# A third working set for VectorE's exponentials, and the scheduler's pace set anew

## The chip, the cores and the metric

The kernel runs on one core of a Trainium2 chip. The metric is the device time of one execution in microseconds (us); lower is better. The engines are called as in the profile: PE (TensorE), ACT (ScalarE), DVE (VectorE), POOL (GpSimd) and SP (SyncE, which issues all DMAs here).

## The reference

Two layers, each an attention block and a dense block, over one sequence of 2048 tokens of width 448, with weights shared by the layers:

```python
def _A_ref(x, wqkv, wo):          # H = 16 heads of Dh = 28
    qkv = (x @ wqkv).reshape(B, S, 3, H, Dh)...
    scores = jnp.einsum("bhqd,bhkd->bhqk", q, k) * Dh ** -0.5
    p = _softmax(scores, axis=-1)
    o = jnp.einsum("bhqk,bhkd->bhqd", p, v)
    return o.transpose(0, 2, 1, 3).reshape(B, S, D) @ wo

def _B_ref(x, w1, b1, w2, b2):    # F = 1792
    r = jnp.maximum(jnp.einsum("bsd,df->bsf", x, w1) + b1, 0)
    return jnp.einsum("bsf,fd->bsd", r * r, w2) + b2

x = A_x                           # (1, 2048, 448) bf16
x = x + _A_ref(_layernorm(x), A_wqkv, A_wo)
x = x + _B_ref(_layernorm(x), B_w1, B_b1, B_w2, B_b2)
x = x + _A_ref(_layernorm(x), A_wqkv, A_wo)
x = x + _B_ref(_layernorm(x), B_w1, B_b1, B_w2, B_b2)
```

## The kernel before

**Units and groups.** The scores are computed with keys on the partitions. A unit is a 128 x 512 tile of scores of one head in one bank of PSUM: two key blocks of 128 by 256 queries, or four by 128 for the last two query blocks of layer 1. There are 2048 units. `s_stream` takes them in threes; a group's scores (`sc`, 128 x 1536, two buffers) are filled by PE (line 882), and `e_stream` has ACT write their exponentials to a probability tile `pt` in bf16 (line 907; `NPT` = 11 buffers of 128 x 1536). `p_stream` multiplies the probabilities with V into `oT` (line 1057). V's spare columns hold ones, so the row sums come along, and `norm_pair` or `norm_turn` divides by them.

**VectorE's thirds.** Where `apart` allows it, the third unit of a group goes to DVE, and ACT's exponential is 128 x 1024. `a_unit` and `a_rest` need four DVE instructions: take (line 965, scores from PSUM to integers), power (line 980, the exponent part), square and close (lines 987 and 995, the polynomial of the fraction, and the product to bf16). They need a working set. `R_v` holds two: one of tiles of its own (`v_i`, `v_e`, `v_h`), the other in parts of the key tiles that are unused at the time (shown as `K_sb<-K_sb`), where the square is written over the integers. The second is there for query blocks 2 to 6 of layer 0 and for layer 1. The close writes to a buffer outside the group: a tile `pd`, or unused blocks of `V_sb` or tiles `h`; `pd_free` lists them, and `held` counts how many are promised.

**The rest.** An opening computes layernorm, Q, K and V block by block between the first groups (`first_block`; the passes are cut as `OPENING` says). When a query block is done, `chain` runs its output projection, layernorm, both products of the dense block (hidden products at line 606 into `r`, squares, then 14 products with `w2`) and adds the result to `x_sb` (line 1193); layer 0's chain ends in the next layer's Q, K and V, layer 1's in a store (line 1281). `heat` puts products with an identity on PE (line 1311), and `s_stream` repeats score products, where PE would otherwise have little to do.

**What sets the order.** Nothing is ordered at run time. A planner keeps modelled clocks for the engines, and from all streams takes again and again the operation that could start first (the order of the streams' priorities on a tie). So constants change the order of instructions on every engine. The constants that count here: `BUSY` and `LOW` (the modelled share of DVE, over `SPAN` us, above which no third is given to it), `TB` and `TB2` (the same for its backlog), `behind` with `L0E`, `L0N`, `L1E`, `L1N` and `MARGIN` (how far the chains must have come by a given unit; when they are behind, the tighter limits hold), `NEAR`, `KEEP`, `LAG` (when banks are left to the chains, when a late third is waited for, where in a pass it may be taken from).

Of the kernel before, what the change touches and what calls it, by code (L numbers as in the profile page):

```python
# [39 lines left out]
OWN = 2  # L40
HALF = 320
L0E = 1310
L0N = 7.6
L1E = 1980
L1N = 6.2
MARGIN = 3.5
LOW = 0.95
TURNS = 1
ENDU = 100
# [10 lines left out]
WINDOW = 2.8  # L60
C_PRIO = 1.6
V_PRIO = 8.5
V_LATE = 4.6
V_LAST = 3
V_AGE = 6
V_PAST = 5
OWN3 = 0
FIRST = 50
V_FIRST = 9
V_WAIT = 3.5  # L70
NEAR = 6
FAR = 17
KEEP = 5
LAG = 5
LEAD = 15
LAST = 690
BUSY = 1.01
TB = 3.6
TB2 = 0.9
SPAN = 8  # L80
NPT = 11
NOS = 2
AEND = 0
# [153 lines left out]
def kernel(  # L237
# [34 lines left out]
    vp = ctx.enter_context(tc.tile_pool(name="vp", bufs=1))  # L272
    osp = ctx.enter_context(tc.tile_pool(name="osp", bufs=NOS))
    np_ = ctx.enter_context(tc.tile_pool(name="np_", bufs=2))
    sp = ctx.enter_context(tc.tile_pool(name="sp", bufs=6))
    dp = ctx.enter_context(tc.tile_pool(name="dp", bufs=NOS, space=bass.MemoryType.DRAM))
    ps_sc = ctx.enter_context(tc.tile_pool(name="ps_sc", bufs=2, space=bass.MemoryType.PSUM))
    ps_m = [ctx.enter_context(tc.tile_pool(name=f"ps_m{i}", bufs=1, space=bass.MemoryType.PSUM)) for i in range(2)]
# [4 lines left out]
    R_r, R_xt, R_os, R_xn, R_on, R_rec = Res(2), Res(3), Res(NOS), Res(2), Res(2), Res(2)  # L283
    R_h = [Res(2), Res(2)]

    R_v = (Res(1), Res(1))


    R_pd = [*[Res(1) for _ in range(5)], Res(NHP), *[Res(1) for _ in range(2)]]
# [476 lines left out]
    def sets_of(unit):  # L766

        pi, kb, r, hh = unit
        l, qb, *_ = passes[pi]
        if l == 0:  # L770
            return R_v if 2 <= qb <= 6 else R_v[:1]
        return R_v

    def apart(i, now, us, soon=SOON):

        if len(units) - i < STOP or not LEAD <= len(gbuf) <= LAST:
            return None
        l, qb = passes[units[i][0]][:2]
        if sum(r.when() is not None and r.when() <= now + soon for r in sets_of(units[i])) <= (0 if soon else pending[0]):
            return None  # L780
        j = i
        if i + LAG > ends_at[units[i][0]]:
            j = ends_at[units[i][0]] + 1
            while j in taken:
                j += 1
            if j >= len(units):
                return None
            rows = {u[3] for u in us}
            js = [k for k in range(j, j + 4) if k < len(units) and k not in taken and units[k][3] not in rows]
            j = js[0] if js else j  # L790
        if passes[units[j][0]][0] != passes[us[0][0]][0]:
            return None
        if held[0] + 1 > min(sum(r.n for r in pd_free(units[k])) for k in (i, j)):
            return None
        if any(pl.tok.get(d) is None or pl.tok[d].end + LAT["DVE"] > now for d in needs(units[j])):
            return None
        if pl.load(SPAN, "DVE") > (LOW if behind(i) else BUSY):
            return None
        if max(0.0, pl.clock["DVE"] - now) + left[0] > (TB2 if behind(i) else TB):
            return None  # L800
        return j
# [16 lines left out]
    def s_stream():  # L818
        while at[0] < len(units):
            gi = len(gbuf)  # L820
            js = ahead(3)
            us = [units[j] for j in js]
            gbuf.append({"n": len(us)})

            def fn(e, gi=gi, us=us, js=js):
                sc = ps_sc.tile([P, 3 * 512], DT.float32, name="sc", tag="sc")
                gbuf[gi]["sc"] = sc
                dst = [sc[:, k * 512:k * 512 + 512] for k in range(len(us))]
                ks = list(range(len(us)))

                def next_at(j):
                    at[0] = j
                    rest = ahead(1)
                    at[0] = rest[0] if rest else len(units)
                    return rest
                own, j = True, None
                if OWN3 and bank_free(o.start) and next_at(js[-1] + 1):
                    j = apart(at[0], o.start, us)
                elif len(us) == 3 and THIRD:
                    own = False  # L840
                    next_at(js[1] + 1)
                    j = apart(at[0], o.start, us[:2], 0.0)
                if j is None:
                    next_at(js[-1] + 1)
                else:
                    if not own:
                        us, ks = us[:2], ks[:2]
                        gbuf[gi]["n"] = 2
                    us, ks = us + [units[j]], ks + [3]
                    taken.add(j)  # L850
                    held[0] += 1
                    pending[0] += 1
                    next_at(at[0])
                    if own:
                        x = gbuf[gi]["x"] = Op("PE", 0.0, None)
                        x.res = min((r for r in R_m if r.when() is not None), key=lambda r: r.when())
                        x.turn = len(x.res.rel)
                        x.res.rel.append(None)
                        dst.append(bank(x, "mt"))
                    else:  # L860
                        x = gbuf[gi]["x"] = o
                        o.need = 2
                    pl.spawn(C_PRIO, a_unit(gi, x, dst[-1], us[-1], passes[us[0][0]][0]))
                for k, (pi, kb, r, hh) in zip(ks, us):
                    where.setdefault((pi, kb), []).append((gi, k, hh))
                    if len(where[pi, kb]) == G:
                        pl.tok["u", pi, kb] = o

                short = (HOT if len(units) - at[0] > ENDU else HOTE) - pl.load(HWIN)
                again = 0  # L870
                if short > 0 and gi > 0:
                    last = ("e" in gbuf[gi - 1] and gbuf[gi - 1]["e"].end) or pl.clock["ACT"] + 1.35
                    again = max(0, min(MORE, int(min(o.room, last - LAT["PE"] - 0.05 - o.end) / 0.22)))
                o.more = 0.22 * again
                for i in list(range(4)) * (again + 1):
                    for k, (pi, kb, r, hh) in enumerate(us):
                        if i >= r:
                            continue
                        l, qb, g, *_ = passes[pi]
                        t0, nt = blocks[l][qb]  # L880
                        rows = slice(DHP * hh, DHP * hh + DHP)
                        nc.tensor.matmul(dst[k][:, i * nt * P:(i + 1) * nt * P],  # L882
                                         lhsT=K_sb[l][rows, g, (kb + i) * P:(kb + i + 1) * P],
                                         rhs=Q_sb[rows, g, t0 * P:(t0 + nt) * P],
                                         start=True, stop=True, tile_position=(DHP * hh, 0))
            o = gbuf[gi]["s"] = Op("PE", 0.20 + 0.01 * max(u[2] for u in us), fn,
                                   deps=list({d for u in us for d in needs(u)}), acq=R_sc, mode="row", sets=("s", gi))
            yield o
        s_left.clear()
        pl.tok["send"] = o  # L890
# [7 lines left out]
    def e_stream():  # L898
        gi = 0
        while gi < len(gbuf) or s_left:  # L900
# [3 lines left out]
            def fn(e, gi=gi, n=n):  # L904
# [3 lines left out]
                                         scale=float(np.log(2.0)) * 2.0 ** -FRAC)  # L908
                if gbuf[gi].get("x") is gbuf[gi]["s"]:
                    apart_from(gi, t)  # L910
            o = gbuf[gi]["e"] = Op("ACT", n / 1200 + 0.066, fn, deps=[("s", gi)], acq=R_pt, need=n // 512,
                                   rel=gbuf[gi]["s"], sets=("e", gi))
            yield o
            gi += 1
# [20 lines left out]
            return V_sb[0][:, 8 + i, :, :].rearrange("p h r -> p (h r)")  # L935
        return hp.tile([P, QB], DT.bfloat16, name="h")[:, :]

    v_i = const.tile([P, 512], DT.int32, name="v_i")
    v_e = const.tile([P, 512], DT.int32, name="v_e")
    v_h = const.tile([P, 512], DT.float32, name="v_h")  # L940

    def set_of(res, l):

        k = R_v.index(res)
        two = lambda a: a.rearrange("p (a n) -> p a n", a=2)
        if k == 0:
            i, e, h = two(v_i[:, :]), two(v_e[:, :]), two(v_h[:, :])
        else:
            keys = K_sb[1 - l][:, :, S - 512:S] if l == 0 else K_sb[0][:, :, 0:512]
            i, e = keys[:, 0:2, :].bitcast(DT.int32), keys[:, 2:4, :].bitcast(DT.int32)  # L950
            h = i.bitcast(DT.float32)
        return i, e, h, two

    def a_unit(gi, x, src, unit, l):
        yield Op("-", 0.0, None, deps=[("s", gi)])
# [19 lines left out]
    def a_rest(gi, c, box, unit):  # L975
# [10 lines left out]
        def square(e):  # L986
            nc.vector.scalar_tensor_tensor(out=box["h"], in0=box["f"], scalar=lin, in1=box["f"],  # L987
                                           op0=ALU.add, op1=ALU.mult)
        h = Op("DVE", 0.684, square, deps=[c] if c.res is R_v[0] else [c, p])
        yield h  # L990
        left[0] -= 0.6

        def close(e):
            pd = gbuf[gi]["pd"] = pd_of(o)
            nc.vector.scalar_tensor_tensor(out=box["two"](pd), in0=box["h"], scalar=low, in1=box["e"].bitcast(DT.float32),  # L995
                                           op0=ALU.add, op1=ALU.mult)
        o = Op("DVE", 0.683, close, deps=[p, h], acq=lambda: pd_free(unit), rel=c, sets=("x", gi))
        gbuf[gi]["x"] = o
        yield o
        left[0] -= 0.6  # L1000
# [6 lines left out]
    def p_stream():  # L1007


        for pi, (l, qb, g, kbs, first, last) in enumerate(passes):  # L1010
# [18 lines left out]
            while todo:  # L1029
# [16 lines left out]
                def fn(e, now=now, begin=begin, close=close, box=box, pi=pi, l=l, g=g, r=r, n=n):  # L1046
                    if "t" not in box:
                        p_next[0] = None
                        box["t"] = bank(box["o"], "oT")
                    held[0] -= sum(k == 3 for kb in now for _, k, _ in where[pi, kb])  # L1050
                    for kb in now:
                        for i in range(r):
                            for gi, k, hh in where[pi, kb]:
# [10 lines left out]
                o = Op("PE", 0.04 + 0.22 * len(now), fn,  # L1064
                       deps=[*by, *{("V", l, kb + i) for kb in now for i in range(r)}],
                       acq=None if "o" in box else pools_now(),
                       rel=[gbuf[gi][w] for w, gi in by], mode="col")
                box.setdefault("o", o)
                yield o
            if last and quick(l, qb, g):  # L1070
# [291 lines left out]
```

## Time and profile before

| | |
|---|---|
| median of 3 runs | 863.42 us (863.35 to 865.34) |
| the profiled execution | 863.88 us, of which its span is 862.1 us |
| granted TensorE clock | 1.00 over the span |
| busy in the span | ACT 842.1 us, PE 817.5, DVE 797.1, POOL 42.8 |
| DMA | 17.97 MB, mean 21 GB/s |

The span runs from the first to the last instruction; 1.78 us of the profiled execution lie around it. Lines of the profile name a source line, an engine, an operation, the tile written and the tiles read, with sizes in partitions x elements. The busy time of a group is the union of its instructions: where one starts before its neighbour ends, the overlap is counted once, so the mean duration times the count can exceed it.

### The profile page before, as it was taken

The page shows a single profiled execution, that of the slowest core. Times are in us where ns is not written, and L with a number is a line of the kernel's source. Part 1 is how long each engine was busy: PE and PEld are TensorE (multiplying, and loading weights), DVE is VectorE, ACT ScalarE, POOL GpSimd, SP SyncE. Part 2 cuts the span into 40 slices and gives each one's busy share as a digit, 9 for nine tenths or more (in the row PEclk, how much of TensorE's full clock was granted, in tenths as well). Part 3 has the DMA queues.
Part 4 walks back from the last instruction along what each step waited for, and adds up shares of the span by engine and source line. Part 5 has one row for each costly group of instructions (what it writes and reads, how often), then busy time and mean ns, then how long its engine had stood idle before and what let it go on. Part 6 is the DMA issues. An engine that isn't in the chain of part 4 may idle for free.

```text
span 862.1 us, 28421 instructions
## 1 busy us (share of the span) xinstructions
PE 817.5 (95%) x12444; PEld 439.2 (51%) x12444; DVE 797.1 (92%) x1644; ACT 842.1 (98%) x702; POOL 42.8 (5%) x95
## 2 busy tenths in 40 slices
PE   8999999999999999999999999899999999999998
PEld 4455555554545545455544554444554444545565
DVE  7998899999999999989889999999999999999663
ACT  8998999999999999999999999999999999999993
POOL 3100000000000000000000000010000000000000
PEclk9999999999999999999999999999999999999999
DMA  9100000000000000000000000011100000000000
GB/s 256 56 3 2 22 21 14 15 15 15 11 6 16 15 14 16 13 5 14 2 3 2 2 2 2 16 28 28 33 9 20 20 26 14 26 20 9 19 3 23
DMA packets 32312, 17.97 MB, mean 21 GB/s; under 512 B 17786, under 2 KB 31739, under 8 KB 32188
## 3 DMA queue, kind: packets, MB, share of 16 engines
q1 hardware_dynamic: 32188, 16.16, 6.7%
q8 instruction: 97, 1.59, 0.8%
q14 instruction: 27, 0.22, 0.1%
HBM read 13.87 MB, written 2.06 MB: 18 GB/s over the span
## 4 chain that ended last, share of the span: by engine, by line
ACT 68%; PE 12%; issue 11%; DVE 6%; DMA 1%; POOL 0%; SPq 0%; ACTq 0%; DVEq 0%
ACT pt L907 68%; PE mt L606 5%; PE sc L882 3%; PE oT L1057 2%; PE sc L606 1%; PE mt L1311 1%; DVE r L1253 1%; DVE K_sb L965 1%; DVE st L460 1%; DMA rec<-scr 1%; DVE K_sb L987 0%; DVE V_sb L995 0%; DVE v_i L965 0%; DMA scr<-dn 0%; DMA V_sb<-in_A_wqkv_dram 0%
## 5 line engine op out<-in xcount | busy, mean ns | idle before, releaser
L907 ACT ACTIVATE pt<-sc 128x1536 bf16<-128x1536 f32 (+1 forms) x683 | 829.6, 1490 | 4.1 <-PE sc L882 4.0
L882 PE MATMUL sc<-Q_sb,K_sb 32*128 32x256 bf16 (+1 forms) x5432 | 307.8, 265 | 32.6 <-ACT pt L907 26.2
L882 PEld LDWEIGHTS <-K_sb 32*128 32x128 bf16 x5432 | 138.0, 92 | 211.1 <-issue 171.7
L1057 PE MATMUL oT<-pt,V_sb 128*32 128x256 bf16 (+1 forms) x3930 | 151.3, 268 | 1.6 <-ACT pt L907 1.4
L606 PE MATMUL mt<-xnT,w 128*128 128x256 bf16 (+1 forms) x896 | 120.1, 271 | 1.4 <-DVE r L1253 0.2
L1057 PEld LDWEIGHTS <-V_sb 128*32 128x32 bf16 x4352 | 91.7, 96 | 46.9 <-issue 44.0
L606 PEld LDWEIGHTS <-w 128*128 128x128 bf16 x952 | 78.0, 98 | 37.7 <-issue 29.2
L965 DVE TENSOR_SCALAR v_i<-sc 128x512 int32<-128x512 f32 x117 | 80.1, 685 | 6.5 <-PE sc L882 5.9
L987 DVE SCALAR_TENSOR_TENSOR v_h<-v_i 128x512 f32<-128x512 uint16 x117 | 79.9, 683 | 0.0
L1253 DVE TENSOR_SCALAR r<-mt 128x512 bf16<-128x512 f32 x106 | 72.6, 685 | 5.0 <-PE mt L606 4.5
L965 DVE TENSOR_SCALAR K_sb<-sc 128x512 int32<-128x512 f32 x90 | 61.7, 686 | 5.4 <-PE sc L882 4.6
L606 PE MATMUL mt<-w,V_sb 128*128 128x448 bf16 (+1 forms) x274 | 66.3, 348 | 0.0
L987 DVE SCALAR_TENSOR_TENSOR K_sb<-K_sb 128x512 f32<-128x512 uint16 x90 | 61.7, 685 | 1.0 <-PE mt L606 0.2
L1311 PE MATMUL mt<-xn,ident 128*128 128x448 bf16 x176 | 58.6, 356 | 1.2 <-DVE xn L570 0.3
L487 POOL TENSOR_TENSOR ve<-mv,eps_t 128x2 f32<-128x2 f32 (+1 forms) x34 | 12.8, 375 | 801.6 <-DVE mv L465 801.6
L980 DVE TENSOR_SCALAR v_e<-v_i 128x512 int32<-128x512 int16 x117 | 49.1, 419 | 0.6
L995 DVE SCALAR_TENSOR_TENSOR V_sb<-v_h,v_e 128x512 bf16<-128x512 f32 x68 | 46.6, 686 | 0.4
L1193 DVE TENSOR_TENSOR x_sb<-x_sb,mt 128x448 bf16<-128x448 bf16 (+1 forms) x61 | 37.0, 611 | 7.0 <-PE mt L606 6.9
L1057 PE MATMUL oT<-V_sb,V_sb 128*32 128x256 bf16 x238 | 42.5, 276 | 0.0
L460 DVE BATCH_NORM_STATS2 st<-x_sb 128x6 f32<-128x448 bf16 x62 | 38.1, 617 | 0.6 <-DMA x_sb<-in_A_x_dram 0.5
L980 DVE TENSOR_SCALAR K_sb<-K_sb 128x512 int32<-128x512 int16 x90 | 37.9, 421 | 0.5
L606 PEld LDWEIGHTS <-V_sb 128*128 128x128 bf16 x302 | 24.7, 97 | 25.2 <-issue 11.2
(104 smaller groups left out, 758.9 us busy)
## 6 DMA issues: line engine op xcount, KB each, us to landing
rec<-scr SPq DMA_DIRECT2D x54, 128.0 KB
x_sb<-in_A_x_dram SPq DMA_DIRECT2D x8, 224.0 KB
out_dram<-x_sb SPq DMA_DIRECT2D x15, 112.0 KB
w<-in_B_w_dram SPq DMA_DIRECT2D x1, 1568.0 KB
w<-in_B_w_dram SPq DMA_DIRECT2D x1, 1344.0 KB
dn<-oT_sb SPq DMA_DIRECT2D x54, 4.0 KB
V_sb<-in_A_wqkv_dram SPq DMA_DIRECT2D x4, 168.0 KB
scr<-dn SPq DMA_DIRECT2D x27, 8.0 KB
```

What stands on the lines that cost most here:

```text
L460: nc.vector.bn_stats(out=box["st"][:, :], in_=x_sb[:, t0 + j, :] if src is None else src())
L606: nc.tensor.matmul(box["t"][:, c0:c0 + n], lhsT=lhsT() if callable(lhsT) else lhsT, rhs=rhs, start=a, stop=b)
L882: nc.tensor.matmul(dst[k][:, i * nt * P:(i + 1) * nt * P], lhsT=K_sb[l][rows, g, (kb + i) * P:(kb + i + 1) * P], rhs=Q_sb[rows, g, t0 * P: ...
L907: t = nc.scalar.activation(out=pt[:, 0:n], in_=gbuf[gi]["sc"][:, 0:n], func=AF.Exp, scale=float(np.log(2.0)) * 2.0 ** -FRAC)
L965: t = nc.vector.tensor_scalar(out=box["i"], in0=two(src), scalar1=EXP_BIAS, scalar2=EXP_LOW, op0=ALU.add, op1=ALU.max)
L980: nc.vector.tensor_scalar(out=box["e"], in0=box["n"], scalar1=2.0 ** 22, scalar2=EXP_BASE, op0=ALU.mult, op1=ALU.add)
L987: nc.vector.scalar_tensor_tensor(out=box["h"], in0=box["f"], scalar=lin, in1=box["f"], op0=ALU.add, op1=ALU.mult)
L995: nc.vector.scalar_tensor_tensor(out=box["two"](pd), in0=box["h"], scalar=low, in1=box["e"].bitcast(DT.float32), op0=ALU.add, op1=ALU.mult)
L1057: nc.tensor.matmul(box["t"][DHP * hh:DHP * hh + DHP, 0:n], lhsT=V_sb[l][:, kb + i, 4 * g + hh, :], rhs=p[:, c0:c0 + n], start=begin and kb ...
L1193: nc.vector.tensor_tensor(out=x_sb[:, tb, lo:hi], in0=x_sb[:, tb, lo:hi], in1=t[:, 0:hi - lo], op=ALU.add)
L1253: nc.vector.tensor_scalar(out=r[:, 0:w], in0=t[:, 0:w], scalar1=0.0, scalar2=None, op0=ALU.max)
L1311: nc.tensor.matmul(t[:, 0:D], lhsT=ident[:, :], rhs=xns[0][:, 0:D], start=True, stop=True)
```

## The change

`R_v` gets a third set. `v_h` is gone; there are two sets of tiles `v_i` and `v_e` of their own, the square is always written over the integers, and the set in the key tiles is the third. In the opening and in layer 0's query blocks past 6 there are now two sets where there was one. When the third unit belongs to the group's own pass, the close writes to `pt[:, 1024:1536]`, the part of the group's own probability tile that ACT leaves unused; it then waits for the group's exponential, and the tile counts as used until that third, too, has been multiplied with V. Such a third takes no buffer of `pd_free`. The pool of small tiles has 5 buffers of each kind in place of 6. Twelve constants of the planner have new values.

```diff
-L0N = 7.6
-L1E = 1980
-L1N = 6.2
-MARGIN = 3.5
+L0N = 7.2
+L1E = 1900
+L1N = 5.4
+MARGIN = 1.5
...
-V_LATE = 4.6
-V_LAST = 3
+V_LATE = 5.2
+V_LAST = 3.5
...
-NEAR = 6
+NEAR = 4
-KEEP = 5
-LAG = 5
+KEEP = 4
+LAG = 12
...
-BUSY = 1.01
-TB = 3.6
+BUSY = 0.995
+TB = 2.2
...
-SPAN = 8
+SPAN = 11
...
-    sp = ctx.enter_context(tc.tile_pool(name="sp", bufs=6))
+    sp = ctx.enter_context(tc.tile_pool(name="sp", bufs=5))
...
-    R_v = (Res(1), Res(1))
+    R_v = (Res(1), Res(1), Res(1))
...
-            return R_v if 2 <= qb <= 6 else R_v[:1]
+            return R_v if 2 <= qb <= 6 else R_v[:2]
...
-        if held[0] + 1 > min(sum(r.n for r in pd_free(units[k])) for k in (i, j)):
+        if units[j][0] != us[0][0] and held[0] + 1 > min(sum(r.n for r in pd_free(units[k])) for k in (i, j)):
...
-                    held[0] += 1
+                    gbuf[gi]["in"] = not own and units[j][0] == us[0][0]
+                    held[0] += not gbuf[gi]["in"]
...
-            o = gbuf[gi]["e"] = Op("ACT", n / 1200 + 0.066, fn, deps=[("s", gi)], acq=R_pt, need=n // 512,
+            o = gbuf[gi]["e"] = Op("ACT", n / 1200 + 0.066, fn, deps=[("s", gi)], acq=R_pt, need=n // 512 + gbuf[gi].get("in", 0),
...
-    v_i = const.tile([P, 512], DT.int32, name="v_i")
-    v_e = const.tile([P, 512], DT.int32, name="v_e")
-    v_h = const.tile([P, 512], DT.float32, name="v_h")
+    v_i = [const.tile([P, 512], DT.int32, name=f"v_i{k}") for k in range(2)]
+    v_e = [const.tile([P, 512], DT.int32, name=f"v_e{k}") for k in range(2)]
...
-        if k == 0:
-            i, e, h = two(v_i[:, :]), two(v_e[:, :]), two(v_h[:, :])
+        if k < 2:
+            i, e = two(v_i[k][:, :]), two(v_e[k][:, :])
...
-        return i, e, h, two
+        return i, e, i.bitcast(DT.float32), two
...
-        h = Op("DVE", 0.684, square, deps=[c] if c.res is R_v[0] else [c, p])
+        h = Op("DVE", 0.684, square, deps=[c, p])
...
-            pd = gbuf[gi]["pd"] = pd_of(o)
+            pd = gbuf[gi]["pd"] = gbuf[gi]["pt"][:, 1024:1536] if gbuf[gi]["in"] else pd_of(o)
...
-        o = Op("DVE", 0.683, close, deps=[p, h], acq=lambda: pd_free(unit), rel=c, sets=("x", gi))
+        own = gbuf[gi]["in"]
+        o = Op("DVE", 0.683, close, deps=[p, h, ("e", gi)] if own else [p, h], acq=None if own else lambda: pd_free(unit), rel=c, sets=("x", gi))
...
-                    held[0] -= sum(k == 3 for kb in now for _, k, _ in where[pi, kb])
+                    held[0] -= sum(k == 3 and not gbuf[gi]["in"] for kb in now for gi, k, _ in where[pi, kb])
...
-                       rel=[gbuf[gi][w] for w, gi in by], mode="col")
+                       rel=[gbuf[gi]["e" if w == "x" and gbuf[gi]["in"] else w] for w, gi in by], mode="col")
```

More of the change, by code (lines that the diff above doesn't have):

```diff
@@ L950, in set_of @@
             i, e = keys[:, 0:2, :].bitcast(DT.int32), keys[:, 2:4, :].bitcast(DT.int32)
-            h = i.bitcast(DT.float32)
-        return i, e, h, two
+        return i, e, i.bitcast(DT.float32), two
     def a_unit(gi, x, src, unit, l):
```

## The prediction

> **What bounds the kernel.** I read the page first, then the groups with shapes kept apart, ScalarE's timeline, the timeline of its one long gap, the chain of waits at the end, and the busy table by stretches.
>
> ```profile
> PE 817.5 (95%) x12444; PEld 439.2 (51%) x12444; DVE 797.1 (92%) x1644; ACT 842.1 (98%) x702; POOL 42.8 (5%) x95
> L907 ACT ACTIVATE pt<-sc 128x1536 bf16<-128x1536 f32 (+1 forms) x683 | 829.6, 1490 | 4.1 <-PE sc L882 4.0
> ...
> L907 ACT ACTIVATE pt<-sc 128x1536 bf16<-128x1536 f32 x475 | 686.3, 1618 | 1.4 <-PE sc L882 1.4
> L907 ACT ACTIVATE pt<-sc 128x1024 bf16<-128x1024 f32 x208 | 238.9, 1196 | 2.6 <-PE sc L882 2.6
> ```
>
> ScalarE (ACT) carries 683 exponentials: 475 of three units, 208 of two, the third unit of those going to VectorE (DVE). Neighbours overlap, so the mean is no pitch; union and difference of means give it: 1618 - 1196 = 422 ns for a unit, T2 = (829.6 - 475 x 0.422) / 683 = 0.921 us, T3 = 1.343 us. PE's 95% includes filler: 5432 score products where 4352 are needed (1920 units of two, 128 of four), and 176 products with the identity (L1311).
>
> ```profile
> 10.44 10.91 ACT L907 ACTIVATE pt<-sc 128x1536 bf16<-128x1536 f32 x8 [0.61 <-PE sc L882]
> 21.78 39.19 ACT L907 ACTIVATE pt<-sc 128x1536 bf16<-128x1536 f32 x31 [0.43 <-PE sc L882]
> 82.02 58.61 ACT L907 ACTIVATE pt<-sc 128x1024 bf16<-128x1024 f32 x48 [2.62 <-PE sc L882]
> 150.87 692.59 ACT L907 ACTIVATE pt<-sc 128x1536 bf16<-128x1536 f32 x573 [0.34 <-PE sc L882]
> ```
>
> Brackets hold the idle time before a run of exponentials. So the span is 10.44 us before the first, 833.02 us of exponentials with 3.39 us of gaps among them (0.43, 2.62, 0.34), and 18.64 us after the last (843.46 to 862.1). Only these three parts can move. The long gap:
>
> ```profile
> 79.46 0.40 PE L1057 MATMUL oT<-pt,V_sb 128*32 128x256 bf16 x6 [0.88 <-ACT pt L907]
> 79.79 1.05 PE L606 MATMUL mt<-xnT,wk 128*128 128x256 bf16 x8
> 80.67 0.92 PE L606 MATMUL mt<-wv,xnT 128*128 128x448 bf16 x4
> 80.87 0.69 DVE L629 CAST K_sb<-mt 128x512 bf16<-128x512 f32 x1 [0.42 <-PE mt L606]
> 81.52 0.61 PE L882 MATMUL sc<-Q_sb,K_sb 32*128 32x256 bf16 x12
> ```
>
> The last opening block's keys come too late: transposes, key product, DVE's copy and scores follow each other while ACT idles. The end:
>
> ```profile
> 852.89 2.04 PE sc L606 x15
> 854.93 0.84 PE mt L606 x15
> 855.77 2.85 PE sc L606 x15
> ...
> 855.81 0.29 DVE L1193 TENSOR_TENSOR x_sb<-x_sb,mt 128x128 bf16<-128x128 bf16 x1 [0.35 <-PE mt L606]
> 858.64 0.62 DVE L1193 TENSOR_TENSOR x_sb<-x_sb,sc 128x448 bf16<-128x448 bf16 x1 [2.55 <-PE sc L606]
> ```
>
> The chain is PE without a break from 843.65. Behind the last block's own two output pieces (320 and 128 columns) stands a whole 448-column output tile of another block.
>
> **Part by part.** The order of the built changed kernel's instructions gives counts and places; prices are rows of before. The new pace constants act only through that order.
>
> Exponentials on ACT: 470 of three and 213 of two. DVE's thirds go from 207 to 212, no more, in spite of a third set. ACT: 5 x 0.422 = 2.1 us less, on the path. DVE: four instructions at 0.60, 0.34, 0.60, 0.60 us from start to start, 5 x 2.14 = 10.7 us more. The cover is DVE's idle time among the exponentials:
>
> ```profile
> 10.44:843.46 833.02, 794.46 (x12215) 423.48 (x12211) 783.11 (x1598) 829.56 (x683) 37.32 (x80) 1.00 0.07 18
> ```
>
> 833.02 - 783.11 = 49.9 us (the fifth figure is DVE). Cost nothing; without that cover, up to 10.7.
>
> Start: the first 14 exponentials, and all that stands between them on every engine, are unchanged. 10.44 and the 0.43 us gap stay.
>
> The 2.62 us gap: before, between the 54th and 55th exponential stand 6 transposes, 16 oT products, 8 key, 4 value and 7 score products, about 2.7 us of PE for one exponential of 1.34 (0.107 us for 256 columns, 0.19 for 448, a quarter of 0.107 for an oT product, a third for a score). In the changed order that block's transposes and key product stand several exponentials earlier, and past the 14th no interval holds over 0.43 us more PE work than its exponential lasts (31st: 1.35 against 0.92; 84th: 1.70 against 1.34, with 12 filler repeats). Before, such excesses cost from nothing to 0.43. I take 0.5 us of new small gaps: 3.4 becomes 0.9, -2.4 us. The bounds are -3.4 (no gap left) and 0 (the gap comes back elsewhere).
>
> The end: the whole tile (15 products) stands ahead of block 15's transposes, where PE otherwise waits for that block's layernorm; its store is off the end too. The last piece is then the 128-column one: the last add ends at 856.10 instead of 859.26, -3.16 us. Hidden-layer products after the last exponential go from 96 to 88 (0.056 us each by "849.65 1.79 PE sc L606 x32" of the chain, -0.45), but behind the transposes PE has one product instead of 16 while DVE copies them, so some 0.3 us of idling comes in. Together -3.3; bounds -3.9 (no idling, less ahead) and -2.8 (transposes held up behind 13 output products). The 2.84 us from the last add to the span's end stay: again one store.
>
> Third set, in-place square: before, 117 squares went to a tile of their own (v_h), 90 were in place; now all 212 are, and wait for the power on their own engine.
>
> ```profile
> 259.84 0.42 DVE L980 TENSOR_SCALAR K_sb<-K_sb 128x512 int32<-128x512 int16 x1
> 260.29 0.69 DVE L987 SCALAR_TENSOR_TENSOR K_sb<-K_sb 128x512 f32<-128x512 uint16 x1
> ...
> 262.26 0.42 DVE L980 TENSOR_SCALAR v_e<-v_i 128x512 int32<-128x512 int16 x1
> 262.60 0.69 DVE L987 SCALAR_TENSOR_TENSOR v_h<-v_i 128x512 f32<-128x512 uint16 x1
> ```
>
> In place it is 0.45 us from power to square, else 0.34: up to 122 x 0.11 = 13.4 us more on DVE. But the changed order puts a power right ahead of its own square 21 times, as often as before in place; elsewhere another operation fills the wait. I take 0, with 13.4 as the bound inside DVE's slack. The Trainium skill (VectorE: DVE Perf Modes, "The DRAIN you can't avoid") says that a semaphore between chained VectorE operations costs nothing extra; by that the 13.4 would be 0 even side by side. The two pairs above disagree, 0.45 against 0.34, and the row stands.
>
> Closing into the group's pt tile: 86 of the 212 thirds. The close waits for the group's ACT exponential; behind it on DVE stand evictions that PE waits for. In the changed order 2 to 7 exponentials start between a group's own and its close, so ACT is long done. Before, close follows take by 3 us or more (261.06 to 264.66 for one); 0; at worst each pays a wait like the one above, 86 x 0.11 = 9.5 us on DVE, again inside 49.9 - 10.7.
>
> Semaphore instructions: DVE 128 to 174, ACT 640 to 652, 21 and 17 ns each by their rows; ACT already has 628 of them ahead of exponentials and no gap: 0. No DMA and no POOL instruction is added; the smaller ring of small tiles (6 to 5) can hold a reciprocal or a DMA on SP, whose queue idles most of the span: 0.
>
> Sum: -2.1 - 2.4 - 3.3 = -7.8. The profiled execution took 863.88 (span 862.1 and 1.78 around it): 856.1. The median, 863.42, lies 0.46 lower: 855.6. I say 856.0.
>
> **Rivals.** (1) The gap comes back: the 31st or 84th interval, or one where DVE is late, idles ACT 2 to 3 us. For it: before's first 100 exponentials have DVE at 92%, the changed order's at 97% by the same pitches. Against: the excesses above. -2.1 - 3.3: 858.5. (2) DVE binds, or the change does little beyond its five units: the 13.4 and 9.5 us land on DVE in stages already full (changed, 51st to 100th exponential: 59.9 of 60.8 us), evictions come late, scores too. Against: before had 59.4 of 60.0 us between the 151st and 200th, without a gap. Some 5 to 6 us of new idling leave about 2 us of gain: 861.5. (3) Slower: ACT waits for pt buffers. There are 11; a group's pt is now held until the third inside it is multiplied. In order of issue 18 pts (before: 10) are read last ten exponentials after their own, one ahead of reuse. ACT's waits name only PE sc today, so the ten cost nothing, with about 1 us in hand each. If PE runs later than its order there, ACT stops. It decides from 7.8 + 2.6 = 10.4 us, or 0.58 us on each of the 18; at 0.65, 11.7 us: 867.8 is the price with every pt late and all else as forecast.
>
> **How the numbers follow.** About 0.3%, 2.6 us, is what a measurement here can tell from no change. Forecast 0.71, (1) 0.14, (2) 0.08, (3) 0.07. Faster by over 0.3% (below 860.8): 0.85; within: 0.08; slower: 0.07. Low end: -2.1 - 3.4 - 3.9 = -9.4, from the median 854.0. High end: gap back and the tail at its worst, -2.1 - 2.8 = -4.9, 859.0, and 1 us of DVE waits: 860.0. (2) and (3) lie outside.
>
> **What would show it.** Right: exponentials 470 + 213 with a union near 827.4; no ACT gap over 1 us between 10.4 us and the last one; the last exponential ending near 839; 15.3 us from there to the end, the last two DVE adds of 320 and 128 columns; ACT waiting for no pt. Wrong: an ACT gap of 2 us or more, one by "PE oT" or DVE (3), DVE over 99% in a stage with gaps beside it (2), or PE idle over 1 us behind block 15's transposes.

## The result, and the profile after

The changed kernel takes 856.67 us (median of 4 runs, 855.66 to 857.27) against 863.45 us; the ratio is 0.9915, 95% interval 0.9897 to 0.9933. That is 6.8 us less. Executions of either kernel fall into two groups 1.4 to 1.9 us apart (the changed kernel's 855.66 and 856.12 against 857.23 and 857.27, the kernel before's 863.35 to 863.49 against 865.34), and a median mixes them, so that the 6.8 us are 7.5 us between the lower groups and 8.1 us between the upper ones. The profiled execution took 856.12 us, its span is 854.3 us, 7.8 us under the 862.1 us of before.

The page, first part, and the group of exponentials with shapes kept apart:

```profile
PE 815.9 (95%) x12350; PEld 435.1 (51%) x12350; DVE 804.3 (94%) x1665; ACT 839.5 (98%) x701; POOL 40.3 (5%) x95
L908 ACT ACTIVATE pt<-sc 128x1536 bf16<-128x1536 f32 (+1 forms) x683 | 827.7, 1454 | 2.0 <-PE sc L883 1.9
...
L908 ACT ACTIVATE pt<-sc 128x1536 bf16<-128x1536 f32 x470 | 673.2, 1583 | 1.1 <-PE sc L883 1.0
L908 ACT ACTIVATE pt<-sc 128x1024 bf16<-128x1024 f32 x213 | 236.9, 1168 | 0.9 <-PE sc L883 0.9
```

The counts are those of the order, 470 and 213, and the union fell from 829.6 to 827.7 us. The waits named for its exponentials are for scores (1.9 of 2.0 us); neither `oT` nor VectorE stands among the releasers. ScalarE's timeline, brackets again the idle time ahead of a run:

```profile
10.54 10.92 ACT L908 ACTIVATE pt<-sc 128x1536 bf16<-128x1536 f32 x8 [0.61 <-PE sc L883]
21.89 31.55 ACT L908 ACTIVATE pt<-sc 128x1536 bf16<-128x1536 f32 x25 [0.43 <-PE sc L883]
53.60 238.53 ACT L908 ACTIVATE pt<-sc 128x1024 bf16<-128x1024 f32 x197 [0.16 <-PE sc L883]
292.39 55.50 ACT L908 ACTIVATE pt<-sc 128x1024 bf16<-128x1024 f32 x46 [0.25 <-PE sc L883]
348.07 3.71 ACT L908 ACTIVATE pt<-sc 128x1024 bf16<-128x1024 f32 x3 [0.19 <-PE sc L883]
352.07 487.60 ACT L908 ACTIVATE pt<-sc 128x1024 bf16<-128x1024 f32 x404 [0.28 <-PE sc L883]
```

The 2.62 us gap near 80 us is gone; five gaps of 0.16 to 0.43 us are left. The last exponential ends at 839.67 (352.07 + 487.60). The end, timeline of PE and VectorE behind it:

```profile
844.50 0.39 PE L510 MATMUL tp<-ident,xn 128*128 128x128 bf16 x4
844.73 0.35 PE L606 MATMUL mt<-w,V_sb 128*128 128x448 bf16 x1
845.41 1.95 PE L606 MATMUL sc<-xnT,w 128*128 128x128 bf16 x32 [0.33 <-DVE xnT L522]
850.77 0.49 DVE L1193 TENSOR_TENSOR x_sb<-x_sb,sc 128x320 bf16<-128x320 bf16 x1 [1.08 <-PE sc L606]
851.61 0.29 DVE L1193 TENSOR_TENSOR x_sb<-x_sb,sc 128x128 bf16<-128x128 bf16 x1 [0.35 <-PE sc L606]
```

The 128-column piece is last and no full-width tile follows. PE idles 0.33 us behind the transposes, where before it had products to do. VectorE, by the table of stretches, over all but the last 0.7 us of the exponentials (VectorE's busy time is the fifth figure):

```profile
10.40:839.00 828.60, 795.48 (x12154) 421.37 (x12147) 790.78 (x1621) 827.05 (x683) 34.79 (x80) 1.00 0.07 19
```

VectorE is busy for 790.8 of 828.6 us, where it was 783.1 of 833.0 before: fuller, but with 37.8 us to spare.

### The profile page after: what moved, and what is told of

Its sections match the earlier page's. It is cut to its first block, busy times and chain, and to the rows that moved or that the text cites. A ratio compares the mean times of both kernels' runs of the same rounds, so it can differ in the third digit from the quotient of the medians.

```text
span 854.3 us, 28309 instructions
## 1 busy us (share of the span) xinstructions
PE 815.9 (95%) x12350; PEld 435.1 (51%) x12350; DVE 804.3 (94%) x1665; ACT 839.5 (98%) x701; POOL 40.3 (5%) x95
## 4 chain that ended last, share of the span: by engine, by line
ACT 37%; PE 34%; DVE 19%; issue 8%; DMA 1%; SPq 0%; ACTq 0%; DVEq 0%
ACT pt L908 37%; PE mt L606 15%; PE sc L883 11%; PE oT L1057 5%; DVE v_i L964 3%; DVE v_i L986 2%; DVE pt L994 2%; PE mt L1311 1%; DVE K_sb L964 1%; DVE r L1253 1%; DVE v_e L979 1%; DVE V_sb L994 1%; DVE K_sb L986 1%; PE sc L606 1%; DVE x_sb L1193 1%
## 5 line engine op out<-in xcount | busy, mean ns | idle before, releaser
L908 ACT ACTIVATE pt<-sc 128x1536 bf16<-128x1536 f32 (+1 forms) x683 | 827.7, 1454 | 2.0 <-PE sc L883 1.9
L964 DVE TENSOR_SCALAR v_i<-sc 128x512 int32<-128x512 f32 x152 | 103.6, 682 | 5.7 <-PE sc L883 5.2
L986 DVE SCALAR_TENSOR_TENSOR v_i<-v_i 128x512 f32<-128x512 uint16 x152 | 103.1, 680 | 0.6
L606 PE MATMUL mt<-w,V_sb 128*128 128x448 bf16 x274 | 68.5, 355 | 0.0
L979 DVE TENSOR_SCALAR v_e<-v_i 128x512 int32<-128x512 int16 x152 | 62.2, 414 | 0.5
L964 DVE TENSOR_SCALAR K_sb<-sc 128x512 int32<-128x512 f32 x60 | 41.0, 684 | 3.3 <-PE sc L883 3.2
L994 DVE SCALAR_TENSOR_TENSOR pt<-v_i,v_e 128x512 bf16<-128x512 f32 x61 | 41.6, 682 | 0.6
L1193 DVE TENSOR_TENSOR x_sb<-x_sb,mt 128x448 bf16<-128x448 bf16 x61 | 37.2, 611 | 4.5 <-PE mt L606 4.3
L986 DVE SCALAR_TENSOR_TENSOR K_sb<-K_sb 128x512 f32<-128x512 uint16 x60 | 40.8, 680 | 0.2
L994 DVE SCALAR_TENSOR_TENSOR V_sb<-v_i,v_e 128x512 bf16<-128x512 f32 x53 | 36.0, 680 | 0.2
L606 PE MATMUL mt<-wo,oTn 128*128 128x448 bf16 x124 | 30.7, 355 | 0.1
```

Of the source, the lines that this page charges most:

```text
L606: nc.tensor.matmul(box["t"][:, c0:c0 + n], lhsT=lhsT() if callable(lhsT) else lhsT, rhs=rhs, start=a, stop=b)
L908: t = nc.scalar.activation(out=pt[:, 0:n], in_=gbuf[gi]["sc"][:, 0:n], func=AF.Exp, scale=float(np.log(2.0)) * 2.0 ** -FRAC)
L964: t = nc.vector.tensor_scalar(out=box["i"], in0=two(src), scalar1=EXP_BIAS, scalar2=EXP_LOW, op0=ALU.add, op1=ALU.max)
L979: nc.vector.tensor_scalar(out=box["e"], in0=box["n"], scalar1=2.0 ** 22, scalar2=EXP_BASE, op0=ALU.mult, op1=ALU.add)
L1193: nc.vector.tensor_tensor(out=x_sb[:, tb, lo:hi], in0=x_sb[:, tb, lo:hi], in1=t[:, 0:hi - lo], op=ALU.add)
```

## The experiments

Theory A is the prediction's account: the time is start + exponentials by count + gaps where PE's work in an interval is too much + what the order leaves behind the last exponential, plus 1.8 us around the span. The rivals change from run to run and stand with each.

**The pace alone, the structure alone, and each half of the structure.** The first two runs split the change:

```diff
# e1_pace_only: the kernel before, with
-L0N = 7.6
+L0N = 7.2
# ... and the other eleven new constants, nothing else
# e2_struct_only: the changed kernel, with
-L0N = 7.2
+L0N = 7.6
# ... and the other eleven old constants, nothing else
# e3_two_sets: the changed kernel, with
-    R_v = (Res(1), Res(1), Res(1))
+    R_v = (Res(1), Res(1))
-            return R_v if 2 <= qb <= 6 else R_v[:2]
+            return R_v if 2 <= qb <= 6 else R_v[:1]
-        if k < 2:
+        if k < 1:
# e4_no_pt_close: the changed kernel, with
-        if units[j][0] != us[0][0] and held[0] + 1 > min(...):
+        if held[0] + 1 > min(...):
-                    gbuf[gi]["in"] = not own and units[j][0] == us[0][0]
+                    gbuf[gi]["in"] = False
```

> The kernel before with the twelve new constants alone: two working sets, no close into pt. Counts of its order: 202 thirds (481 exponentials of three units, 202 of two), no interval between exponentials with more than 0.54 us of PE work over its exponential, and 24 instead of 28 full-width output products behind the last exponential, the last full tile still at the very end. Theory A (time = start + exponentials by count + gaps by overfull intervals + what is left behind the last exponential): 10.5 + 832.1 + about 1.2 of gaps + about 17.7 + 1.8 = 863.3, so the vanished 2.6 us gap is paid for by five units fewer on VectorE. Rival B (the new constants are the gain, the sets and the close only enable them): 857 to 859.

Measured: 863.73 us, ratio 1.0003 (0.9994 to 1.0011) to the kernel before. Theory A holds and B falls: the long gap is gone here too (gaps 1.8 us less) and the end is 1.4 us shorter, but five units fewer on VectorE make the exponentials 2.8 us longer. One detail of the expectation was wrong: the last full tile does not stand at the very end, its add starts at 856.23 us, ahead of those of 320 (858.26) and 128 columns (859.10).

> The changed kernel with the twelve old constants: three sets, close into pt. Counts: 226 thirds (457 + 226), 19 more than before, so exponentials of 822.1 us; but at the boundary of the layers (430th exponential) one interval holds 28 output products, a layernorm's transposes, key and value products and the scores that need them, 7.3 us of PE work over its exponential plus VectorE and POOL steps in a row; 32 full-width output products stand behind the last exponential. Theory A: a gap of 9 to 11 us there, 2 to 4 us of others, an end of about 19.3: 865 to 869, slower than before although ScalarE has 7.5 us less to do. Rival B (structure is the gain: ScalarE's sum decides): 855 to 857. Rival C (the constants matter little): within 1 us of the changed kernel.

Measured: 876.43 us, ratio 1.0151 (1.0137 to 1.0164). The direction is A's, B and C fall; the size is 7 to 11 us beyond A's. ScalarE's union is only 823.2 us, but it idles 23.1 us in all: 13.7 us in one gap at the boundary of the layers, where A had 9 to 11, and 9.4 us in a dozen others of up to 2.04 us, where A had 2 to 4. Timeline of that place, PE, VectorE and ScalarE, and then the table of stretches (the last three figures are the granted clock, the DMA share and GB/s):

```profile
543.82 0.70 DVE L570 TENSOR_SCALAR xn<-x_sb,mv,rstd 128x448 bf16<-128x448 bf16 x2 [1.08 <-POOL rstd L488]
544.27 0.70 PE L510 MATMUL tp<-ident,xn 128*128 128x128 bf16 x8 [2.88 <-DVE xn L570]
545.76 1.87 PE L606 MATMUL mt<-xnT,wk 128*128 128x256 bf16 x8 [0.78 <-DVE xnT L522]
549.05 1.03 PE L883 MATMUL sc<-Q_sb,K_sb 32*128 32x256 bf16 x12
549.76 1.94 ACT L908 ACTIVATE pt<-sc 128x1024 bf16<-128x1024 f32 x2 [13.70 <-PE sc L883]
```

```profile
541.00:544.20 3.20, 0.39 (x3) 0.00 (x0) 1.81 (x5) 0.00 (x0) 1.06 (x4) 1.00 0.00 0
544.20:545.70 1.50, 0.70 (x8) 0.51 (x9) 1.01 (x3) 0.00 (x0) 0.00 (x0) 0.72 0.00 0
545.70:549.00 3.30, 3.24 (x12) 1.57 (x11) 0.70 (x2) 0.00 (x0) 0.00 (x0) 0.50 0.00 0
551.50:555.00 3.50, 3.27 (x52) 1.60 (x51) 3.27 (x7) 2.71 (x4) 0.00 (x0) 0.98 0.03 7
```

In this order the last chain of layer 0 comes so late that layer 1's first scores have to wait for it: sums, layernorm, transposes, keys, scores in a row. The kernel differs from the changed one in the constants alone, so the gap is their doing. That the thirds make VectorE late there is not shown: from 380 to 536 us it is busy for 151.8 of 156 us, in the changed kernel, which has no such gap, for 153.4.

PE idles 2.88 us in the gap. The granted clock is still 1.00 when the transposes begin at 544.27, falls to 0.50 near 544.9 and is back near 551.7 (by stretches of 0.1 us), and eight key products take 1.87 us where they take 1.05 in the stall of the kernel before. With the value products (1.70 against 0.92) and the scores (1.03 against 0.61) the lower clock makes an estimated 2 us of the 13.7. The Trainium skill (TensorE: Matmul & The Clock Gate, "Part 1: The HAM clock gate") names an idle window of about 3.4 us for the fall to half rate. The trace does not contradict it: the fall comes some 3.5 us after the last product ahead of the idling (541.04 + 0.35), with only the transposes between. Nothing in this study keeps PE busy there, so that the idling is the cause of the lower clock is read, not shown.

> The changed kernel without the third set: one set of own tiles and the one in the key tiles, as before; close into pt and new constants kept. Counts: 205 thirds (478 + 205), an interval of 1.05 us over at the 299th exponential, more work behind the last exponential (112 hidden and 15 full-width output products instead of 88 and 14). Theory A: 10.5 + 831.0 + about 2.9 + 16.8 + 1.8 = 863.0, about as before. Rival B (a third set only adds waiting thirds, without need): as the changed kernel, 856 to 857.

Measured: 868.03 us, ratio 1.0055 (1.0042 to 1.0068). B falls; A is 5 us short. The profiled execution, 866.68 us, lies 1.3 us under the median; in it the exponentials hold 832.4 us, 1.4 more than A worked out from their count, the gaps 5.1 instead of 2.9, and the end 17.1. The largest gap stands behind the 299th exponential, the interval that the count had 1.05 us over; ScalarE and PE there:

```profile
379.41 0.61 PE L510 MATMUL tp<-ident,xn 128*128 128x128 bf16 x8 [1.08 <-DVE r L1253]
379.95 0.61 PE L883 MATMUL sc<-Q_sb,K_sb 32*128 32x256 bf16 x12
380.65 2.79 ACT L908 ACTIVATE pt<-sc 128x1536 bf16<-128x1536 f32 x2 [2.48 <-PE sc L883]
```

PE's transposes wait 1.08 us for an eviction on VectorE, and the scores stand behind them in PE's queue. Such a wait does not show in a count of PE's work per interval; here it comes on top of the excess.

> The changed kernel with its closes sent to the old buffers and never into pt; three sets and new constants kept. Counts: 206 thirds (477 + 206), the intervals and all that stands behind the last exponential as in the changed kernel. Theory A: seven units more on ScalarE at 0.422 us each, nothing else: 856.7 + 3.0 = 859.6 against the changed kernel's median (859.1 against its profiled run). Rival B (holding pt longer, or waiting for the group's exponential, costs the changed kernel something): at or below 856.7 in spite of the seven units. Rival C (the close into pt is most of the gain): 862 or more.

Measured: 859.91 us, ratio 0.9962 (0.9950 to 0.9974). A's number is 859.6; B and C fall. The medians are 3.2 us apart, near the 3.0 us of seven units at 0.422 us. The profiled executions are 3.8 us apart (859.89 against 856.12, where A has 859.1): exponentials 3.2 us, gaps 0.4 us (1.8 against 1.4), the end the same. So the agreement to 0.3 us is partly luck of the medians.

**One term at a time.** One constant each, chosen because the built order changes in one of the three parts; and the in-place square with an unchanged order:

```diff
# e5_end_alone: the kernel before, with
-LAG = 5
+LAG = 12
# e6_gap_back: the changed kernel, with
-SPAN = 11
+SPAN = 8
# e7_square_in_place: the kernel before, with
-            i, e, h = two(v_i[:, :]), two(v_e[:, :]), two(v_h[:, :])
+            i, e, h = two(v_i[:, :]), two(v_e[:, :]), two(v_i[:, :]).bitcast(DT.float32)
# e8_span14: the changed kernel, with
-SPAN = 11
+SPAN = 14
```

> The kernel before with one constant changed, LAG = 12. Counts: 207 becomes 207 thirds (476 + 207, so one exponential of three units for one group boundary: 0.4 us more on ScalarE); the opening's overfull interval at the 54th exponential is the same as before; what stands behind the last exponential is what the changed kernel has there (88 hidden and 14 full-width output products, the 128-column piece last). Theory A: the end is worth 3.3 to 4.0 us by itself and the gap near 80 us stays: 863.4 + 0.4 - 3.7 = 860.1 (859.6 to 860.6). Rival B (the end follows from the third set, or the work moved ahead of the last exponential is paid for there): 862.5 to 864.

Measured: 861.19 us, ratio 0.9972 (0.9963 to 0.9981): faster than before by the end alone, with the gap in place:

```profile
82.21 462.84 ACT L907 ACTIVATE pt<-sc 128x1024 bf16<-128x1024 f32 x382 [2.62 <-PE sc L882]
```

From the last exponential (844.32) to the end of the span (859.0) it is 14.7 us instead of 18.6. The total is 0.6 us beyond A's range, but still outside B's. The spans hardly show the miss: the exponentials are 0.5 us longer (A had 0.4), start and gaps 0.2 us each, and the profiled executions differ by 3.1 us (863.88 to 860.77). The medians differ by 2.3 us, because this kernel's lies 0.4 us above its profiled execution and that of the kernel before 0.4 us below.

> The changed kernel with one constant put back, SPAN = 8. Counts: 210 thirds (473 + 210), the end as in the changed kernel, but the opening's overfull interval is back at the 54th exponential, 2.2 us over by the prices of PE's products, with the transposes, two key products, a value product and the scores in one interval. Theory A: 3 units x 0.42 = 1.3 us more of exponentials and a gap of about twice the excess (before: 1.3 over gave 2.6), 3.5 to 4.5 us, near 80 us: 856.7 + 1.3 + 4.0 = 862.0 (861 to 863). Rival B (the gap's time is made up later, ScalarE's buffers smooth it out): 857.5 to 858.5.

Measured: 861.59 us, ratio 0.9981 (0.9972 to 0.9989) to the kernel before, 4.9 us over the changed kernel. A's total holds, its composition only in part. The gap near 80 us is back:

```profile
81.46 25.40 ACT L908 ACTIVATE pt<-sc 128x1024 bf16<-128x1024 f32 x21 [2.83 <-PE sc L883]
```

It is 2.83 us, not 3.5 to 4.5, and nine others of 0.17 to 0.43 us make up the rest (5.4 us of gaps in all, 4.0 more than in the changed kernel); the exponentials are 2.0 us longer instead of 1.3. Three of these waits, 0.6 us in all, are put down to ScalarE's own `pt`; what stands behind them is open. B falls: the gap is not made up later.

> The kernel before with the square of the first set written over the integers (v_h unused), and nothing else: the order of instructions on every engine is the one of before. 51 of its 117 squares of that set stand right behind their own power, so by the pairs of the trace (0.45 against 0.34 us) VectorE has 51 x 0.11 = 5.6 us more. Theory A: VectorE's 49.9 us of idle time hide it: 863.0 to 864.0. Rival B (VectorE is the second bound, each wait moves an eviction and with it the scores): 866 to 869. By the sentence of the Trainium skill (VectorE: DVE Perf Modes, The DRAIN you can't avoid) that a semaphore between chained operations costs nothing extra, the pairs would stay at 0.34 us.

Measured: 863.78 us, ratio 1.0002 (0.9993 to 1.0011). The pair of power and square, VectorE's timeline:

```profile
107.65 0.42 DVE L980 TENSOR_SCALAR v_e<-v_i 128x512 int32<-128x512 int16 x1
108.10 0.69 DVE L987 SCALAR_TENSOR_TENSOR v_i<-v_i 128x512 f32<-128x512 uint16 x1
```

It is now 0.45 us from start to start; at the same place of the kernel before it is 0.33 (107.39 to 107.72), and the 51 such pairs of the two traces have these values in the median. VectorE's busy time in the stretch goes from 783.1 to 786.1 us, 3.0 us more where 5.6 were worked out (while it waits, it is not busy), yet the time stays: VectorE's idle time hides it. A holds and B falls. The sentence of the Trainium skill quoted in the expectation does not fit this pair: the wait costs 0.11 to 0.12 us.

> The changed kernel with SPAN = 14 in place of 11. Counts: 214 thirds (469 + 214), intervals and end as in the changed kernel. Theory A: one unit, 0.4 us, less: 856.2, which cannot be told from 856.7. Rival B (more thirds make VectorE late somewhere): 857.5 to 860.

Measured: 859.16 us, ratio 0.9943 (0.9931 to 0.9956), 2.5 us slower than the changed kernel by the medians, 1.5 us by the profiled executions (857.58 against 856.12). A fails, B's range has it. Of the 1.5 us, 0.9 are gaps (2.3 us instead of 1.4), 0.1 to 0.2 exponentials, and 0.4 lie outside the span (2.1 us around it instead of 1.8). B's cause is not shown: the gaps name PE, nearly all of them its scores, and not VectorE.

**The account of all kernels**, each from its own profiled execution (us; gaps are the stretch of the exponentials less their union):

| kernel | start | exponentials | gaps | end | span |
|---|---|---|---|---|---|
| before | 10.4 | 829.6 | 3.4 | 18.6 | 862.1 |
| changed | 10.5 | 827.7 | 1.4 | 14.7 | 854.3 |
| e1 pace only | 10.6 | 832.4 | 1.6 | 17.3 | 861.8 |
| e2 structure only | 10.6 | 823.2 | 23.1 | 18.9 | 875.8 |
| e3 two sets | 10.4 | 832.4 | 5.1 | 17.1 | 864.9 |
| e4 no close into pt | 10.6 | 830.9 | 1.8 | 14.7 | 858.0 |
| e5 end alone | 10.6 | 830.1 | 3.6 | 14.7 | 859.0 |
| e6 gap back | 10.5 | 829.7 | 5.4 | 14.7 | 860.3 |
| e7 square in place | 10.6 | 829.7 | 3.3 | 18.6 | 862.2 |
| e8 SPAN 14 | 10.6 | 827.9 | 2.3 | 14.7 | 855.4 |

None of the variants beats the changed kernel.

## Why the prediction was right, point by point

- **Start, 0.** 10.54 against 10.44 us; the other kernels' starts lie between 10.36 and 10.62 with the same first instructions, so this is from run to run.
- **Exponentials, -2.1.** Measured -1.9, by the counts foretold: 0.37 us for a unit, where 0.42 was taken. In e4 seven units are 3.2 us of exponentials, 0.45 us each.
- **The gap, -2.4.** Measured -2.0 (3.4 to 1.4): the long gap went, and 1.0 us of small ones besides the one at 21.5 us stood in place of the 0.5 assumed. e6 shows the gap coming back where the order has it, and the time not being made up.
- **The end, -3.3.** Measured -4.0 (18.65 to 14.68 by the spans unrounded, 862.10 and 854.35), 0.1 beyond the bound of -3.9. The step that was mis-sized is "The 2.84 us from the last add to the span's end stay": it is 2.45 now (851.90 to 854.35). The rest is -3.6, from 15.80 to 12.23 us between the last exponential and the last add, near the -3.3 worked out. The forecast 0.3 us of idling behind the transposes came (0.33). e5 shows the end as a term of its own: the constant `LAG` alone gives it.
- **VectorE, 10.7 us more at no cost.** Measured 7.7 us more among the exponentials (783.1 to 790.8); what makes it less than 10.7 was not traced. e7 shows that the waits of 51 squares for their powers (3.0 us more of busy time) cost nothing in the order of before. In e3's largest gap VectorE does cost: there an eviction stands between a PE queue and its scores.
- **The close into pt, 0.** e4 sends the closes elsewhere, gains nothing and loses seven units; no exponential names a wait for a pt, before or after. The rival of held buffers fell.
- **The rivals.** No gap of 2 us came back, and VectorE is at 95% with 37.8 us of idling. The sum of -7.8 is the span's difference to the tenth, but that is luck: gaps 0.4 and exponentials 0.2 short of their forecast and a start 0.1 later are made up by an end 0.7 better.

What the prediction left out is that neither half of the change is worth anything alone. The twelve constants by themselves leave the time as it was (e1, ratio 1.0003), the structure by itself costs 13 us (e2). One constant by itself does gain: `LAG` (e5). The third set is worth 11.4 us under the new constants (e3 against the changed kernel; 10.6 by the profiled executions), and yet it stands for seven thirds only, some 3 us; gaps (3.7 us) and end (2.4 us) differ by more than that. It is the planner's order as a whole that changes. No run varies the smaller pool of small tiles, or the in-place square in the changed order.

## What to carry to other kernels

Where one engine runs without a break, divide the span at its first and last instruction: start, its own work by count, its gaps, and the end. Start, counts and what stands at the end can be read from a built order before it runs; of the gaps only a part. More work moved off the bound engine is a gain only while the order still brings the rest in time: e2 had the shortest exponentials of all and was the slowest kernel. A count of work per interval finds where several products pile up (the long gaps of the kernel before, e2, e3 and e6 stand where it has them), but not a short wait for another engine in the middle of a queue. The gaps came out 0.5 us above the forecast in the changed kernel, 2.2 in e3 and 8 to 12 in e2, so a forecast from counts needs such a margin.

## What the runs showed of the hardware

- A final store of 128 columns left 2.4 to 2.5 us between the last add and the end of the span in all seven kernels that end with one (the changed kernel, e1, e3 to e6, e8), one of 448 columns 2.8 us in the kernel before and e7 and 2.6 in e2 (872.54 + 0.62 to 875.8).
- In e2 PE had no product for 2.88 us, then eight transposes, then none for 0.78 us. Its granted clock went from 1.00 to 0.50 near 544.9 us, during the transposes, and was back near 551.7, 5.9 us after the key products had begun at 545.76.
- A 128x512 square that waits for the power directly ahead of it on VectorE starts 0.45 us after it, one that does not 0.34 us (e7 and the kernel before).
